# A fifth block of hidden gradients turned by a transposing load, and three PSUM copies moved from VectorE to ScalarE

## The chip, the cores and the metric

The kernel runs on one core of a Trainium2 chip. The metric is the device time of one execution in microseconds (us). The engines are named as in the profile: PE is TensorE's matmul stream and PEld its weight loads, DVE is VectorE, ACT is ScalarE, POOL is GpSimd, SP is SyncE, which here only issues DMAs; SPq is SP's queue, the instructions that SP works through in order. L1062 is line 1062 of the kernel file.

## The reference, cut to what matters

The function is the sum of its input, a gated convolution and a bilinear feed-forward block, and the kernel computes the output and all nine gradients.

```python
def _fwd_reference(A_q, A_k, A_v, A_shift_k, A_ssm_k, A_ssm_D, B_x, B_w_gate, B_w_up, B_w_down):
    # S = 2048 rows, D = 512 columns, F = 1376 hidden columns, bfloat16
    def _A_ref(q, k, v, shift_k, ssm_k, ssm_D):
        k_shift = sum(k_pad[:, t:t + S, :] * shift_k[:, 3 - t] for t in range(4))   # a 4-tap shift
        kv = k_shift * v
        y = irfft(rfft(kv) * rfft(ssm_k)) + kv * ssm_D                              # a long convolution
        return q * y
    def _B_ref(x, w_gate, w_up, w_down):
        return ((x @ w_gate) * (x @ w_up)) @ w_down
    xn = _layernorm(A_q)
    return A_q + _A_ref(xn, A_k, A_v, A_shift_k, A_ssm_k, A_ssm_D) + _B_ref(xn, B_w_gate, B_w_up, B_w_down)

out, vjp = jax.vjp(f, A_q, A_k, A_v, A_shift_k, A_ssm_k, A_ssm_D, B_w_gate, B_w_up, B_w_down)
return (out, *vjp(grad_out))
```

Of the outputs, these matter here: the weight gradients of the feed-forward block (out_7, out_8: D x F; out_9: F x D), the gradient of the four taps (out_4: 512 x 4), that of ssm_D (out_6: 512) and that of ssm_k (out_5).

## The kernel before, in words

The program has two halves. In the first (up to about 313 us of the profile) the feed-forward block is computed in eight chunks of 256 rows, and the convolution's spectra beside it. For each chunk the kernel keeps h (the product of gate and up) and the gradients dg and du, laid with the hidden columns on the partitions: three tiles of 128 hidden columns x 256 rows for each of the 11 blocks of hidden columns (ten of 128 and one of 96). Seven of the eight chunks go to the DRAM buffer HDD; the last stays on the chip in `hds[1]`.

The second half is the one that the change touches. Its backbone is `dw`, a loop over the 11 blocks `fb` (numbered from 0, so that `fb` 6 is the seventh and `fb` 8 the ninth). For each block `down_grad` multiplies h, turned so that rows lie on the partitions, with the output's gradient (`pd`, L1026, 16 matmuls; out_9), and then `pu` (L1062, 64 matmuls; out_7 and out_8) multiplies the normalized input with dg and du, turned as well. So each block needs 48 squares of 128 x 128 turned: h, dg and du, each with 16 groups of 128 rows. There are two ways to do it:

- `load_hb` loads a block as it lies into a buffer `hb`, and `hid_t(fb, t)` turns it on PE in three steps t = 0, 1, 2, each 16 transposes into a PSUM tile `pt` (L859) and one ACT copy into `nath` or `natd`. Steps 0 and 1 come ahead of the block's `pu`, right after the `down_grad` of the block before; step 2 sits in the middle of `down_grad` of the block itself.
- For the blocks in `TURNED`, before the change `fb` 7 to 10, `load_t` issues a transposing DMA from HDD into `natT` (L817). Only the last chunk is turned on PE, in `last_t`: 6 transposes (L829) and one ACT copy into a small tile `nat7`. `last_t(fb + 1)` comes in the middle of the `pu` of `fb`.

A block's load is issued two blocks ahead, from the middle of `down_grad(fb - 2)`. The buffers: `hb` has two, used in turn (and by `natT` of whole blocks); `natd` has two and `nath` one. The block `SPLIT` puts five chunks of its `natT` into a `natd` and two into the `nath`; the last block of 96 columns goes into a `natd`.

Beside the backbone run four side generators: after each `yield` of `dw` (six for a block, numbered n = 0, 1, 2, ...; block `fb` begins at n = 6 fb) a side whose turn has come does one step. `inv_y` (from n = 0, every third) brings the convolution's results back with `pq` and computes with DVE the products `dks` and `kb`; `dsk_gram` (from n = 27, every second) computes the taps' gradient; `inv_dk` (from n = 35, every third) writes out_5, and `put_dD` out_6; `ew` (from n = 10, every third) does the elementwise end on DVE, alternating `final(b)` and `bwd(b)` for eight row groups. `put_late` at the start of an `ew` step stores what the step before made (`o`, `e`, `dk`), and `final(b)` first loads `bb` of the next group. The tiles `o`, `e`, `dk` and `bb` have two buffers each.

`dsk_gram` makes, for each of four column groups c, a PSUM tile `pk` (L1085, 32 matmuls). DVE multiplies its two halves with an identity mask straight out of PSUM into `kd` (L1091), sums (L1093) and at the end turns the result on PE (`pts`, L1101) and copies it out into `dskt`; both `kd` and `dskt`, like `nat7`, live in the two buffers of the tag `dd`. PSUM has three large tiles (`P2`: `pt`, `pu`, `pk`, `po`, `pq` and others share them) and two small ones (`P1`: `pd`, `pts`, `ptd`). A tile is given to the next user when its copy-out is done.

The order within each engine's queue, SP's too, is planned when the program is built, by the program's order and by readiness in the planner's own model of time; the engines then work through their queues strictly in order. `tc.high_priority(offset=SOON)` lets an instruction go ahead of up to 300 others. `tc.issue_after(x)` puts an instruction behind x on x's queue: `behind(fb)` does so for some of the transposing loads.

Of the kernel before, what the change touches and what calls it, by code (L numbers as in the profile page):

```python
# [9 lines left out]
F32 = mybir.dt.float32  # L10
I32 = mybir.dt.int32
ALU = mybir.AluOpType
ACTF = mybir.ActivationFunctionType
AX = mybir.AxisListType
# [6 lines left out]
R = 16  # L21
P = 128
NC4 = 4
FBLK = [(i * 128, min(128, F - i * 128)) for i in range((F + 127) // 128)]
NFB = len(FBLK)
NCH = 8
SOON = 300
# [163 lines left out]
def kernel(  # L191
# [24 lines left out]
    nc = tc.nc  # L216
# [17 lines left out]
    def act(o, i):  # L234
        nc.scalar.copy(o, i)  # L235

    def dve(o, i):
        nc.vector.tensor_copy(o, i)  # L238
# [13 lines left out]
    def P2(name, shape, dt=F32):  # L252
        return ps2.tile(shape, dt, name=name, tag="p2")

    def P1(name, shape, dt=F32):
        return ps1.tile(shape, dt, name=name, tag="p1")

    ident = const.tile([P, P], BF, name="ident")
# [397 lines left out]
    first = ExitStack()  # L656
# [131 lines left out]
    LG = {}  # L788
# [6 lines left out]

    hbs = {}

    TURNED = range(NFB - 4, NFB)

    def behind(fb):  # L800
        first = {NFB - 2: lambda: LG["bb"], NFB - 1: lambda: LG["og"]}.get(fb)
        return tc.issue_after(first().ins) if first else ExitStack()

    def load_t(fb):

        f0, fw = FBLK[fb]
        if fb == SPLIT:
            parts = ((0, 5, "n", dict(tag="natd", bufs=2)), (5, NCH - 1, "n", dict(tag="nath")))
        elif fw < P:
            parts = ((0, NCH - 1, "n", dict(tag="natd", bufs=2)),)  # L810
        else:
            parts = ((0, NCH - 1, "b", dict(tag="hb")),)
        nats[fb, 0] = {}
        for a, e, pool, kw in parts:
            t = CP[pool].tile([P, e - a, 3, 2, fw], BF, name="natT", **kw)
            with behind(fb) as _, tc.high_priority(offset=SOON):
                nc.sync.dma_start_transpose(out=t[:].rearrange("s c t h f -> s (c t h) f"),  # L817
                                            in_=HDD[:fw, fb, a:e].rearrange("p c t s -> p (c t s)"))
            for c in range(a, e):
                nats[fb, 0][c] = t[:, c - a]  # L820

    SPLIT = NFB - 2

    def last_t(fb):
        f0, fw = FBLK[fb]
        pt = P2("pt7", [P, 3, 2, P], BF)
        for t in range(3):
            for h in range(2):
                nc.tensor.transpose(pt[:, t, h, :fw], hds[1][:fw, fb, t, h * 128:h * 128 + 128], ident[:fw, :fw])  # L829
        n7 = c2b.tile([P, 3, 2, P], BF, name="nat7", tag="dd")  # L830
        act(n7[:, :, :, :fw], pt[:, :, :, :fw])
        nats[fb, 1] = n7

    def nat_h(fb, r):
        f0, fw = FBLK[fb]
        if fb not in TURNED:
            return nats[fb, 0][:, r, :fw]
        return nats[fb, 0][r // 2][:, 0, r % 2, :] if r < R - 2 else nats[fb, 1][:, 0, r % 2, :fw]

    def nat_d(fb, r):  # L840
        f0, fw = FBLK[fb]
        if fb not in TURNED:
            return nats[fb, 1][:, :, r, :fw]
        return nats[fb, 0][r // 2][:, 1:3, r % 2, :] if r < R - 2 else nats[fb, 1][:, 1:3, r % 2, :fw]

    def hid_t(fb, t):
        if fb in TURNED:
            return
        f0, fw = FBLK[fb]
        hb = hbs.pop(fb) if t == 2 else hbs[fb]  # L850
        if t == 0:
            nats[fb, 0] = CP["n"].tile([P, R, P], BF, name="nath")
        elif t == 1:
            nats[fb, 1] = CP["n"].tile([P, 2, R, P], BF, name="natd", bufs=2)
        dst = nats[fb, 0] if t == 0 else nats[fb, 1][:, t - 1]
        pt = P2("pt", [P, R, P], BF)
        for r in range(R):
            hs = hb[:fw, r // 2, t] if r < R - 2 else hds[1][:fw, fb, t]
            nc.tensor.transpose(pt[:, r, :fw], hs[:, (r % 2) * 128:(r % 2) * 128 + 128], ident[:fw, :fw])  # L859
        act(dst[:, :, :fw], pt[:, :, :fw])  # L860
# [56 lines left out]
    c2b = ctx.enter_context(tc.tile_pool(name="c2b", bufs=2, side="right", reuse_waits="tile"))  # L917
# [8 lines left out]
    dsk = c2.tile([P, NC4, 4], F32, name="dsk")  # L926
# [15 lines left out]
    DKS = {}  # L942
# [46 lines left out]
    def inv_dk():  # L989
        o5t = c2.tile([P, NC4, P, R], BF, name="o5t", tag="o5k")  # L990
        o5 = out_5.rearrange("(c q) s -> c q s", q=P)
        for rq in range(4):
            gk = gks.pop(0)
            if rq == 0:
                gk_last = load_gk_last()
            for b in range(2):
                po = P2("po", [P, 2, 4, P])
                for h in range(2):
                    for i in range(4):
                        for c in range(2):  # L1000
                            nc.tensor.matmul(po[:, h, i, :], lhsT=(gk_last(c, i) if rq == 3 else gk[:, c, i])[:, cs(2 * b + h)], rhs=TB.IW[:, c, :],
                                             start=(c == 0), stop=(c == 1))
                act(o5t[:, 2 * b:2 * b + 2, :, 4 * rq:4 * rq + 4], po[:].rearrange("q h r s -> q h s r"))
                if b == 1 and rq < 2:
                    gks.append(load_gk(2) if rq == 0 else None)
                if rq == 3:
                    for c in (2 * b, 2 * b + 1):
                        nc.sync.dma_start(o5[c], o5t[:, c].rearrange("q s r -> q (s r)"))
                yield
            if rq == 0:  # L1010
                yield from put_dD(o5t)

    def put_dD(o5t):
        act(dDs[:], o5t[:, :, 0, 0])
        yield
        pt = P1("ptd", [P, P], BF)
        nc.tensor.transpose(pt[:NC4, :], dDs[:], ident[:])
        dDt = c2.tile([NC4, P], BF, name="dDt")
        dve(dDt[:], pt[:NC4, :])
        nc.sync.dma_start(out_6.rearrange("(c p) -> c p", p=128), dDt[:])  # L1020

    def down_grad(fb):
# [18 lines left out]
    def load_h(fb):  # L1041
        (load_t if fb in TURNED else load_hb)(fb)

    def dw():
        og = None
        load_hb(2)
        for fb, (f0, fw) in enumerate(FBLK):
# [12 lines left out]
            for c in range(NC4):  # L1060
# [3 lines left out]
                if c == 1:  # L1064
                    yield
                    if fb + 1 in TURNED:
                        last_t(fb + 1)
# [11 lines left out]
    def dsk_gram():  # L1079
        for c in range(NC4):  # L1080
            pk = P2("pk", [P, 2, D])
            for r in range(R):
                for h in range(2):
                    c0 = c * 128 + 64 * h
                    nc.tensor.matmul(pk[64 * h:64 * h + 64, h, 0:256], lhsT=dks[:, r, c0:c0 + 64],  # L1085
                                     rhs=KH[0][:, r:r + 4, c0:c0 + 64], start=(r == 0), stop=(r == R - 1))
            kd = c2b.tile([P, 4, 64], F32, name="kd", tag="dd")
            with tc.high_priority(offset=SOON):
                for h in range(2):
                    hs = slice(64 * h, 64 * h + 64)  # L1090
                    nc.vector.tensor_tensor(kd[hs], pk[hs, h, 0:256].rearrange("q (j c) -> q j c", j=4),  # L1091
                                            ident[hs, hs].unsqueeze(1).to_broadcast((64, 4, 64)), op=ALU.mult)
                nc.vector.tensor_reduce(dsk[:, c, :], kd[:], axis=AX.X, op=ALU.add)  # L1093
            yield
        dskb = c2.tile([P, 4, NC4], BF, name="dskb")
        nc.vector.tensor_copy(dskb[:], dsk[:].rearrange("q c i -> q i c"))
        for _ in range(2):
            yield
        pt = P1("pts", [P, 4, P], BF)
        for j in range(4):  # L1100
            nc.tensor.transpose(pt[:NC4, j, :], dskb[:, 3 - j, :], ident[:])  # L1101
        dskt = c2b.tile([NC4, P, 4], BF, name="dskt", tag="dd")
        dve(dskt[:], pt[:NC4].rearrange("c j q -> c q j"))
        nc.sync.dma_start(out_4.rearrange("(c p) j -> c p j", p=128), dskt[:])
        yield

# [88 lines left out]
    def load_dk():  # L1195
        gks.append(load_gk(0))
        gks.append(load_gk(1))
        yield

    sides = [every(seq(inv_y(), load_dk()), 0, 3), every(dsk_gram(), 27, 2), every(inv_dk(), 35, 3), every(ew(), 10, 3)]  # L1200
    for n, _ in enumerate(dw()):
        for sd in sides:
# [36 lines left out]
```

## Time and profile before

| What | Value |
|---|---|
| Median of three runs | 480.83 us (479.90 to 481.28) |
| The profiled execution's own time | 481.82 us |
| Its span, first to last instruction | 480.0 us |
| Granted PE clock | 0.999 |
| PE busy | 464.5 us, 97% |
| DVE, ACT busy | 340.5 us (71%), 305.6 us (64%) |
| Last PE matmul ends | about 475.9 us into the span |
| Last DVE work of the elementwise end ends | 471.8 us |

The profile is of one execution. Its parts: busy time by engine; the span in 40 slices; the DMA queues; the chain of work that ended last, followed back from the last instruction to what released each step; groups of like instructions; waits (who waited for whom, in us, how often, and the longest); and a timeline of each engine, with the idle time before an instruction in square brackets and what ended it. A DMA issue on SPq is shown with the time that SP was held by it; the time from issue to landing is shown apart.

### The profile page before, as it was taken

The page shows a single profiled execution, that of the slowest core. Times are in us where ns is not written, and L with a number is a line of the kernel's source. Part 1 is how long each engine was busy: PE and PEld are TensorE (multiplying, and loading weights), DVE is VectorE, ACT ScalarE, POOL GpSimd, SP SyncE. Part 2 cuts the span into 40 slices and gives each one's busy share as a digit, 9 for nine tenths or more (in the row PEclk, how much of TensorE's full clock was granted, in tenths as well). Part 3 has the DMA queues.
Part 4 walks back from the last instruction along what each step waited for, and adds up shares of the span by engine and source line. Part 5 has one row for each costly group of instructions (what it writes and reads, how often), then busy time and mean ns, then how long its engine had stood idle before and what let it go on. Part 6 is the DMA issues. An engine that isn't in the chain of part 4 may idle for free.

```text
span 480.0 us, 10366 instructions
## 1 busy us (share of the span) xinstructions
PE 464.5 (97%) x4252; PEld 311.6 (65%) x4293; DVE 340.5 (71%) x609; ACT 305.6 (64%) x349; POOL 14.0 (3%) x30
## 2 busy tenths in 40 slices
PE   7999999999999999999999999999999999999996
PEld 6867755547648447447447743576777687677885
DVE  7889989979366567686777877022257899599893
ACT  4957677659568678779779975375576535233141
POOL 8000000000000000000000000110000000000000
PEclk9999999999999999999999999999999999999999
DMA  8999999989998968968978379999899979999858
GB/s 268 374 381 366 310 296 320 315 300 328 318 288 270 277 202 255 285 200 245 298 235 259 118 272 331 388 329 313 312 361 364 371 260 320 318 267 239 252 155 294
DMA packets 111132, 139.85 MB, mean 291 GB/s; under 512 B 38859, under 2 KB 84336, under 8 KB 109550
## 3 DMA queue, kind: packets, MB, share of 16 engines
q1 hardware_dynamic: 109502, 137.85, 89.7%
q10 hardware_dynamic: 1584, 1.36, 1.0%
q8 instruction: 33, 0.54, 0.5%
q14 instruction: 13, 0.11, 0.1%
HBM read 67.08 MB, written 63.41 MB: 272 GB/s over the span
## 4 chain that ended last, share of the span: by engine, by line
PE 67%; DMA 15%; DVE 14%; issue 2%; SPq 2%; ACT 1%; DVEq 0%; ACTq 0%
PE px L555 15%; PE pgu L512 13%; PE pu L1062 8%; PE py L548 7%; PE pdh L518 6%; PE pd L1026 4%; PE ps L584 3%; DMA khC<-in_A_k_dram 3%; PE pg L613 3%; DMA ssk<-in_A_ssm_k_dram 2%; PE pf L370 2%; PE pt L859 2%; DMA vb<-in_A_v_dram 2%; DMA kb<-KS 2%; DMA x_b<-in_A_q_dram 2%
## 5 line engine op out<-in xcount | busy, mean ns | idle before, releaser
L555 PE MATMUL px<-WT,hd 128*128 128x512 bf16 (+1 forms) x340 | 78.6, 379 | 1.6 <-issue 1.4
L1062 PEld LDWEIGHTS <-xnC 128*128 128x128 bf16 x704 | 67.0, 98 | 8.4 <-issue 0.6
L555 PEld LDWEIGHTS <-hd 128*128 128x128 bf16 (+1 forms) x352 | 32.8, 98 | 44.4 <-issue 7.7
L235 ACT CAST gu<-pgu 128x1024 bf16<-128x1024 f32 (+1 forms) x48 | 45.4, 946 | 16.9 <-PE pgu L512 16.7
L235 ACT CAST GO<-pg 128x1024 bf16<-128x1024 f32 x48 | 46.2, 1015 | 13.8 <-issue 7.2
L235 ACT CAST SP<-ps 128x1024 bf16<-128x1024 f32 x47 | 45.5, 1025 | 13.7 <-PE ps L584 11.8
L512 PE MATMUL pgu<-xt,Wu 128*128 128x256 bf16 (+1 forms) x352 | 53.1, 273 | 1.1 <-DVE kn L238 0.6
L600 DVE TENSOR_TENSOR T<-SP 128x2048 bf16<-128x2048 bf16 x24 | 29.3, 1222 | 34.8 <-ACT SP L235 34.7
L512 PE MATMUL pgu<-xt,Wg 128*128 128x256 bf16 (+1 forms) x352 | 52.8, 273 | 0.0
L1062 PE MATMUL pu<-natd,xnC 128*128 128x256 bf16 x448 | 51.2, 273 | 0.0
L518 PE MATMUL pdh<-gt,WdT 128*128 128x256 bf16 (+1 forms) x352 | 46.9, 273 | 0.1
L235 ACT CAST fst<-pf 128x1024 bf16<-128x1024 f32 x44 | 42.7, 1031 | 5.5 <-issue 2.3
L512 PEld LDWEIGHTS <-Wu 128*128 128x128 bf16 (+1 forms) x352 | 33.0, 100 | 15.6 <-issue 10.7
L548 PE MATMUL py<-Wd,hd 128*128 128x512 bf16 (+1 forms) x167 | 40.2, 379 | 0.8 <-issue 0.5
L235 ACT CAST og<-pu 128x1024 bf16<-128x1024 f32 (+1 forms) x11 | 10.9, 993 | 43.7 <-PE pu L1062 28.3
L518 PEld LDWEIGHTS <-WdT 128*128 128x128 bf16 (+1 forms) x352 | 34.9, 100 | 4.8
L512 PEld LDWEIGHTS <-Wg 128*128 128x128 bf16 (+1 forms) x352 | 34.8, 100 | 3.7
L235 ACT COPY natd<-pt 128x2048 bf16<-128x2048 bf16 x14 | 26.2, 1875 | 12.0 <-PE pt L859 12.0
L533 DVE TENSOR_TENSOR hd<-gu,dh 128x1024 bf16<-128x1024 bf16 (+1 forms) x48 | 30.8, 641 | 0.8
L532 DVE TENSOR_TENSOR hd<-gu 128x512 bf16<-128x512 bf16 (+1 forms) x48 | 19.0, 397 | 16.7 <-ACT gu L235 16.7
L548 PEld LDWEIGHTS <-hd 128*128 128x128 bf16 (+1 forms) x176 | 16.5, 98 | 20.8 <-issue 3.1
L600 DVE TENSOR_TENSOR U<-SP 128x2048 bf16<-128x2048 bf16 x24 | 29.2, 1218 | 0.0
(177 smaller groups left out, 687.4 us busy)
## 6 DMA issues: line engine op xcount, KB each, us to landing
HDD<-hd SPq DMA_DIRECT2D x35, 384.0 KB, 4.5
FD<-fst SPq DMA_DIRECT2D x24, 512.0 KB, 4.9
X<-FD SPq DMA_DIRECT2D x24, 512.0 KB, 5.5
GD<-GO SPq DMA_DIRECT2D x24, 512.0 KB, 3.9
g<-GD SPq DMA_DIRECT2D x11, 1024.0 KB, 8.9
hb<-HDD SPq DMA_DIRECT2D x7, 1344.0 KB, 10.2
bb<-BX SPq DMA_DIRECT2D x8, 512.0 KB, 5.5
BX<-bx SPq DMA_DIRECT2D x7, 512.0 KB, 3.9
```

The source lines that it names most:

```text
L235: nc.scalar.copy(o, i)
L512: nc.tensor.matmul(pgu[:w, i, t, :], lhsT=W[:, c, f0:f0 + w], rhs=xt[:, :, c, :], start=(c == 0), stop=(c == NC4 - 1))
L518: nc.tensor.matmul(pdh[:w, i, :], lhsT=WdT[:, c, f0:f0 + w], rhs=gt[:, :, c, :], start=(c == 0), stop=(c == NC4 - 1))
L532: nc.vector.tensor_tensor(hd[:fw, fb0:fb0 + n, 0, :], gu[:fw, :n, 0, :], gu[:fw, :n, 1, :], op=ALU.mult)
L533: nc.vector.tensor_tensor(hd[:fw, fb0:fb0 + n, 1:3, :], gu[:fw, :n], dh[:fw, :n].unsqueeze(2).to_broadcast((fw, n, 2, 256)), op=ALU.mult)
L548: nc.tensor.matmul(py[:], lhsT=hd[:fw, fb, 0, ss], rhs=Wd[:fw, fb, :], start=(fb == 0), stop=(fb == NFB - 1))
L555: nc.tensor.matmul(px[:], lhsT=hd[:fw, fb, t, ss], rhs=W[:fw, fb, :], start=(t == 1 and fb == 0), stop=(t == 2 and fb == NFB - 1))
L584: nc.tensor.matmul(ps[32 * q:32 * q + 32, a, :], lhsT=TB.EF[64 * a:64 * a + 64, 4 * g + q, ri].rearrange("p k j -> p (k j)"), rhs=X[64 * a ...
L600: tt(W[:].rearrange("p c a d -> p c (a d)"), A[:, i:i + 1].rearrange("p c a d -> p c (a d)").to_broadcast((P, 2, 2 * D)), B[:].rearrange(" ...
L613: nc.tensor.matmul(pg[q // 2][64 * a:64 * a + 64, q % 2, :], lhsT=TB.EI[32 * q:32 * q + 32, 2 * g + a, yi].rearrange("p k c -> p (k c)"), ...
L1026: nc.tensor.matmul(pd[:fw, :], lhsT=nat_h(fb, r), rhs=goC[:, r, :], start=(r == 0), stop=(r == R - 1))
L1062: nc.tensor.matmul(pu[:, c, :, :fw], lhsT=xnC[:, r, cs(c)], rhs=nat_d(fb, r), start=(r == 0), stop=(r == R - 1))
```

## The change

The block `fb` 6 joins `TURNED`: its plain load and its three steps of `hid_t` go, and a transposing load, `last_t(6)` and one more `nat7` come. The split over `natd` and `nath` goes from `fb` 9 to `fb` 8, and `fb` 9 takes a whole `hb` buffer. `behind` gets two more entries: the load of `fb` 6 is placed behind the last load of `kb`, and that of `fb` 8 behind the last load of `load_gk_last`. In `dsk_gram` ACT now copies the two halves of `pk` out of PSUM into `kd` (one tile for two values of c), DVE multiplies in place from there, without the raised priority, and the turning of the result is two steps later (n = 43 rather than 39). The copies of `dskt` and `dDt` out of PSUM are done by ACT rather than DVE.

```diff
-    TURNED = range(NFB - 4, NFB)
+    TURNED = range(NFB - 5, NFB)
 
     def behind(fb):
-        first = {NFB - 2: lambda: LG["bb"], NFB - 1: lambda: LG["og"]}.get(fb)
+        first = {NFB - 5: lambda: DKS["kb", R - 2], NFB - 3: lambda: LG["gk"], NFB - 2: lambda: LG["bb"], NFB - 1: lambda: LG["og"]}.get(fb)
         return tc.issue_after(first().ins) if first else ExitStack()
...
-    SPLIT = NFB - 2
+    SPLIT = NFB - 3
...
         dDt = c2.tile([NC4, P], BF, name="dDt")
-        dve(dDt[:], pt[:NC4, :])
+        act(dDt[:], pt[:NC4, :])
...
-            kd = c2b.tile([P, 4, 64], F32, name="kd", tag="dd")
-            with tc.high_priority(offset=SOON):
-                for h in range(2):
-                    hs = slice(64 * h, 64 * h + 64)
-                    nc.vector.tensor_tensor(kd[hs], pk[hs, h, 0:256].rearrange("q (j c) -> q j c", j=4),
-                                            ident[hs, hs].unsqueeze(1).to_broadcast((64, 4, 64)), op=ALU.mult)
-                nc.vector.tensor_reduce(dsk[:, c, :], kd[:], axis=AX.X, op=ALU.add)
+            if c % 2 == 0:
+                kd = c2b.tile([P, 2, 4, 64], F32, name="kd", tag="dd")
+            for h in range(2):
+                hs = slice(64 * h, 64 * h + 64)
+                act(kd[hs, c % 2], pk[hs, h, 0:256].rearrange("q (j c) -> q j c", j=4))
+                nc.vector.tensor_tensor(kd[hs, c % 2], kd[hs, c % 2], ident[hs, hs].unsqueeze(1).to_broadcast((64, 4, 64)), op=ALU.mult)
+            nc.vector.tensor_reduce(dsk[:, c, :], kd[:, c % 2], axis=AX.X, op=ALU.add)
             yield
...
-        for _ in range(2):
+        for _ in range(4):
             yield
         pt = P1("pts", [P, 4, P], BF)
         for j in range(4):
             nc.tensor.transpose(pt[:NC4, j, :], dskb[:, 3 - j, :], ident[:])
         dskt = c2b.tile([NC4, P, 4], BF, name="dskt", tag="dd")
-        dve(dskt[:], pt[:NC4].rearrange("c j q -> c q j"))
+        act(dskt[:], pt[:NC4].rearrange("c j q -> c q j"))
```

## The prediction

> **What bounds the kernel now.** First the page's busy times: PE works 97% of the span, at a granted clock of 0.999, so the question is what PE still waits for and which of its work goes. The table of stretches then says where the idle is: between 410 and 420 us PE is busy 8.89 of 10 us, the only stretch after 314 us that loses over 0.3 us, before the work runs out.
>
> ```profile
> PE 464.5 (97%) x4252; PEld 311.6 (65%) x4293; DVE 340.5 (71%) x609; ACT 305.6 (64%) x349; POOL 14.0 (3%) x30
> ...
> 410.00:420.00 10.00, 8.89 (x86) 6.42 (x82) 5.22 (x14) 3.20 (x3) 0.00 (x0) 1.00 1.02 338
> ```
>
> Next PE's timeline. These are the three turning steps of `fb` 6 (the second and third wait for DVE, in brackets), and a `last_t` of a block that a transposing load turns:
>
> ```profile
> 400.69 0.94 PE L859 MATMUL pt<-ident,hb 128*128 128x128 bf16 x14
> 401.96 0.96 PE L859 MATMUL pt<-ident,hb 128*128 128x128 bf16 x14 [0.22 <-DVE kd L1091]
> 417.64 0.95 PE L859 MATMUL pt<-ident,hb 128*128 128x128 bf16 x14 [1.06 <-DVE kd L1091]
> 425.07 0.51 PE L829 MATMUL pt<-ident,hd 128*128 128x128 bf16 x6
> ```
>
> The chain of waits around that gap leads from PE through DVE's late `kd` to a late `bb` and to SP, which was held by a transposing load:
>
> ```profile
> 404.92 3.82 SPq L817
> ...
> 410.36 5.54 DMA bb<-BX
> ...
> 416.00 0.69 DVE o L1139
> ...
> 416.72 0.42 DVE kd L1091
> ```
>
> Last SP's queue, and what waited for stores in it. The plain load of `fb` 6 holds SP 0.64 us, the transposing one of `fb` 7 9.69:
>
> ```profile
> 391.28 0.64 SPq L793 DMA_DIRECT2D hb<-HDD  x1
> ...
> 399.05 9.69 SPq L817 DMA_TRANSPOSE natT<-HDD  x1
> ```
>
> ```profile
> 396.31 1.01 ACT L235 CAST og<-pu 128x1024 bf16<-128x1024 f32 x1 [7.90 <-DMA out_dram<-og]
> ```
>
> ```profile
> 413.62 0.69 DVE L1138 TENSOR_TENSOR o<-xnC,yC 128x1024 bf16<-128x1024 bf16 x1 [4.29 <-DMA out_dram<-o]
> ```
>
> So PE sets the end, but SP, held by transposing loads, is what makes DVE and ACT late, and these make PE wait. The change takes work from PE and puts a fifth such load on SP.
>
> **PE's work.** A group of 32 transposes takes 1.79 us in the chain, 0.056 us each. The 48 of `fb` 6 go: 2.69 us. `last_t(6)` adds 6: 0.33 us in the chain for another block. Net -2.35 us, all on PE, which has no cover; it counts in full.
>
> **The gram sums by ACT.** The two waits above (0.22 + 1.06 = 1.28 us) were for a PSUM tile that DVE had not yet read. Both waiting steps are gone, and the tile now comes free by ACT. A copy of 256 elements costs ACT 0.37 us (the half `od`, 96x256); bounds 0.37 and 0.59 (512 elements). I take 0.37, the same length: 8 x 0.37 = 3.0 us. Against that ACT loses three copies of 1.87 us and gains a `nat7` of 0.80, `dskt` (0.64 to 0.80 by the rows of 576 and 768 elements) and `dDt` (0.20, like `dDs`): about a microsecond less in all, on an engine at 20 to 50% there. DVE keeps eight multiplies, 0.42 us each from PSUM; from SBUF I leave them at that (0.3 to 0.45 by the sum's 0.41 over the same length), and loses `dskt` 0.68 and `dDt` 0.20. Cover for the loss of priority: `kd` of c = 1 must be summed before `nat7` of `fb` 6 may take its buffer, about 409 us; in program order it follows `final(3)`, which ended at 403.4, or 409 if DVE is 6 us late. PE needs that `nat7` only at row group 14 of `down_grad(6)`, near 416. Cost 0, a few us if that cover is gone. -1.28 us.
>
> [...]
>
> **The load of `fb` 6, on SP.** It goes behind the last `kb` load (issued 378.79) with raised priority, so I put it ahead of the stores `o`, `e` of group 1 (now 379.32 and 380.39) and of all up to `og`. It needs the buffer that `hid_t(4, 2)` leaves at 381.56. SP is then held 9.06 to 9.69 us (the two whole blocks of 128 in the trace): to 391.3. SP's cover is its own idle, about 7 us ahead of 387.96 and 4.6 ahead of 399.05. What is queued behind, with today's durations: `o`, `e`, `kb`, `dk`, `kb`, `bb` of group 3 by 393.9 (now 390.0), the two `og` stores by 395.0 (now 391.2), `od`, two loads `g` by 397.3 (now 394.4; first used at 413.8, landing in 8.9: covered). So SP is level again when the load of `fb` 7 can start, at 399.05, where its buffer comes free. Landing in about 11 us is far ahead of the use at 413.
>
> Who waits: ACT's `og` copy of `fb` 4 waits for those stores now (396.31); 3.8 us later it ends at 401.1. It holds a PSUM tile, and behind it stand two `kd` copies (0.74) and the `natd` copy of `hid_t(5, 2)` (1.76): done about 403.6. Without the two turning steps PE would begin `pu` of `fb` 5 at 402.6. Cost +1.0 us. The bounds: 0 if the `og` stores stay ahead; 4.3 if the load is put just ahead of `og` and behind `bb`, since then `og` lands near 404.5 and PE's `pk` at 400.7 has no tile. I take 1.0, for the priority.
>
> DVE: the store of `o` of group 1 lands at 391.4 + 4.5 = 395.9 (4.5 is the median of these stores), and DVE's L1138 of group 3 ran at 390.19: 5.7 us late. DVE then idles less at 409 to 416 (4.29 for `o` of group 2, 1.09 for `bb`), so most is made up: +0.3 us at 416.7, less the 0.88 of copies. DVE ends today at 471.8, 4.1 ahead of PE. Cost 0 as long as DVE ends within some 4 us of that.
>
> **The later loads.** `fb` 8 goes straight behind `load_gk_last` (418.2 to 419.2), about where it is (420.41); its two pieces hold SP as long as today's two of `fb` 9 (7.35 + 2.61). It now stands ahead of the store of `o` of group 4 (now 419.32), see the third rival. `fb` 9 as one piece starts after `bb` (433.3 today), lands by 446 and is used at 451; `fb` 10 is unmoved. 0 us each.
>
> **Two more steps of delay.** `pts` moves next to `ptd`, with nothing of PE's between but `po`. `ptd` then needs the small PSUM tile that `od` of `fb` 7 holds for 0.65 us after `down_grad(7)`; `pts` fills 0.33 of it. Today the gap at 432.5 is 0.1. Cost +0.2; bounds 0 and 0.6.
>
> **The sum.** -2.35 - 1.28 + 1.0 + 0.2 = -2.4 us. The profiled execution took 481.82 us (span 480.0); after it, 479.4. The median shown is 480.83, 1.0 below the profiled execution, so on the median: 478.4 us.
>
> [...]
>
> **The rivals.** 1: the stores stay ahead of the load, or its hold costs nobody (SP does idle 7 us there). -2.35 - 1.28 + 0.2 = -3.4: 477.4 us. Against it: the load of `fb` 7 did jump over `o`, `e`, `dk` and `bb` today.
>
> 2: the copies out of PSUM come no sooner, so the release by ACT does not do what it says: ACT stands behind `og` until 404.5. -2.4 + 3.3 = +0.9: 481.7 us, no measurable change (0.3%, 1.4 us, is about what can be told). For it: ACT already waited 7.90 us there.
>
> 3, slower: SP's holds make DVE end last. The price: 5.7 us at 390 by the load of `fb` 6, and 7.3 at 426.5, because `o` of group 4 is stored only when the load of `fb` 8 lets go (428.7) and lands at 433.8; 13.0 us. Off it: 0.9 of copies, 1.7 of today's wait at 447, and of the 5.4 idle at 409 to 416 half, since these stores slip too: 7.7 net, DVE ends at 479.5; its last `dk` needs 3.4 us to land, so the span is 482.9, +2.9: 483.7 us. It decides from DVE's end past 476.6 (480.0 - 3.4). For it: DVE has 99% of busy slices from 420 on. Against: the planner can put other work ahead of a waiting `o`. [...]
>
> **How the numbers follow.** The forecast 0.45, rival 1 0.15, rival 2 0.15, rival 3 0.25. Faster (below 479.4): the first two, 0.60; same: 0.15; slower (above 482.3): 0.25. The forecast's own range is 477.5 to 479.3; the whole one goes from 476.9 (rival 1 with the 0.2 and a little idle gone) to 482.7, which takes in rival 2 and the near edge of 3. No clock matters: it stays at 1.0.
>
> **What would show it.** L859 x16 fewer by three groups, L829 by one more; no PE wait for `kd`. The SP queue: six issues of L817, the first near 381.6, held 9 to 10 us. The ACT `og` copy of `fb` 4 near 400. DVE's L1138 of group 3 waiting for a store; its end between 471 and 474. Wrong it is if DVE ends after PE, if a `natT` lands late for its `pd`, or if `pts` waits for `dskb`.

## The result, and the profile after

The changed kernel takes 483.15 us (median of 12 runs, 480.63 to 486.29) where the kernel before takes 480.00 on the same chip (478.38 to 481.28): a ratio of 1.0063, 95% interval 1.0044 to 1.0081. It is slower, by some 3 us; 478.4 had been forecast, and the time lies above the range (476.9 to 482.7). The profiled execution took 484.33 us, with a span of 482.5 us.

The page's busy times, then the table of stretches (us; busy time of PE, PEld, DVE, ACT and POOL with their instructions; granted PE clock, as a share of full speed; DMA share; GB/s), both of the changed kernel:

```profile
PE 465.4 (96%) x4210; PEld 311.8 (65%) x4251; DVE 339.2 (70%) x607; ACT 304.2 (63%) x357; POOL 13.9 (3%) x30
```

```profile
410.00:420.00 10.00, 9.95 (x93) 7.63 (x92) 7.20 (x20) 4.41 (x6) 0.00 (x0) 1.00 0.99 331
...
440.00:450.00 10.00, 5.96 (x35) 3.77 (x34) 9.93 (x22) 4.13 (x5) 0.00 (x0) 0.71 1.11 268
```

The hole that the change was to close is closed: between 410 and 420 us PE is busy 9.95 us, not 8.89. PE has 42 matmuls fewer (4210 against 4252), which is 48 transposes out and 6 in. And yet PE's busy time has grown, from 464.5 to 465.4 us. The second row shows what is new: between 440 and 450 us PE stands idle for 4 us, and the granted clock is 0.71 on the mean of those 10 us; the matmuls behind the idle are busy for longer than the same ones in the kernel before (the 16 of `po` 1.71 us against 0.89). In the kernel before, this stretch was full:

```profile
440.00:450.00 10.00, 9.95 (x95) 7.63 (x95) 8.26 (x19) 3.53 (x4) 0.00 (x0) 1.00 1.14 259
```

The chain of waits leads through that hole (start, us, what; in order of time):

```profile
438.79 2.31 SPq L817
...
441.20 0.53 SPq L1034
...
441.82 3.07 DMA out_dram<-dskt
...
444.98 0.81 ACT nat L235
...
445.84 1.03 PE pd L1026 x2
446.87 1.71 PE po L1001 x16
448.58 4.73 PE pu L1062 x32
```

Read from the `pd` upwards: the last two matmuls of `down_grad(8)` (L1026) wait for the copy of `nat7` of `fb` 8 (L235); that copy waits for a store of `dskt`, 4 KB, to land; and that store waits in SP's queue behind `od` (L1034) and a transposing load (L817). Here are the two queues, SP's of the changed kernel and ACT's:

```profile
431.69 9.41 SPq L817 DMA_TRANSPOSE natT<-HDD  x1
441.20 0.53 SPq L1034 DMA_DIRECT2D out_dram<-od  x1
441.82 0.29 SPq L1104 DMA_DIRECT2D out_dram<-dskt  x1
```

```profile
429.51 0.57 ACT L235 COPY dskt<-pts 4x512 bf16<-4x512 bf16 x1
...
444.98 0.80 ACT L235 COPY nat<-pt 128x768 bf16<-128x768 bf16 x1 [13.37 <-DMA out_dram<-dskt]
```

`dskt` is copied at 429.51, and its store is issued only at 441.82, since the load of `fb` 9 stands ahead of it and holds SP for 9.41 us. `dskt` and `nat7` share the two buffers of the tag `dd`, so ACT sits idle for 13.37 us (the first 2.8 of them ahead of the end of `nat7`'s own transposes). In SP's queue of the kernel before, the store stood ahead of that load, and `nat7` waited only for its own transposes (SP, then ACT):

```profile
432.61 0.29 SPq L1104 DMA_DIRECT2D out_dram<-dskt  x1
...
433.80 10.00 SPq L817 DMA_TRANSPOSE natT<-HDD  x2
```

```profile
437.71 0.80 ACT L235 COPY nat<-pt 128x768 bf16<-128x768 bf16 x1 [2.81 <-PE pt L829]
```

The loss has two pieces. The first is PE's wait, 4.04 us, here in PE's timeline of the changed kernel and then the same two matmuls in the kernel before:

```profile
445.84 1.03 PE L1026 MATMUL pd<-goC,nat 128*128 128x512 bf16 x2 [4.04 <-ACT nat L235]
```

```profile
444.92 0.59 PE L1026 MATMUL pd<-goC,nat 128*128 128x512 bf16 x2
```

The second is the clock behind it. The stretches of a microsecond in the changed kernel:

```profile
444.00:445.00 1.00, 0.00 (x0) 0.00 (x0) 1.00 (x3) 0.02 (x1) 0.00 (x0) 0.58 1.07 402
...
447.00:448.00 1.00, 1.00 (x12) 1.00 (x11) 1.00 (x2) 1.00 (x2) 0.00 (x0) 0.50 0.92 300
...
450.00:451.00 1.00, 1.00 (x7) 0.69 (x6) 1.00 (x1) 0.00 (x0) 0.00 (x0) 0.51 1.26 166
451.00:452.00 1.00, 1.00 (x11) 0.90 (x10) 0.93 (x3) 0.00 (x0) 0.00 (x0) 1.00 1.94 125
```

From about 444.2 to 451.0 us the granted clock is 0.50, 6.8 us long. In the chain the two `pd` take 1.03 us, `po` 1.71 and `pu` 4.73, where the same groups take 0.59, 0.89 and 3.49 at full clock: 2.5 us more. Together 6.5 us. Up to the hole PE had gained: `down_grad(8)` begins at 438.83 us against 441.90 before, 3.1 us earlier (and about 3.6, since this execution entered the second half some 0.5 us later). 6.5 lost less 3.1 won is 3.4 us, and PE's last matmul ends at 479.24 us against 475.84: 3.4 us later.

These 6.5 us are those of an execution with a mean clock of 0.992. Of the twelve, five were at 0.992 (median 484.8 us), five at 0.996 (482.2) and two at 1.0 (480.63 and 482.2), so the part that the clock takes differs from one execution to the next.

### The profile page after: what moved, and what is told of

Its sections match the earlier page's. It is cut to its first block, busy times and chain, and to the rows that moved or that the text cites. A ratio compares the mean times of both kernels' runs of the same rounds, so it can differ in the third digit from the quotient of the medians.

```text
span 482.5 us, 10288 instructions
## 1 busy us (share of the span) xinstructions
PE 465.4 (96%) x4210; PEld 311.8 (65%) x4251; DVE 339.2 (70%) x607; ACT 304.2 (63%) x357; POOL 13.9 (3%) x30
## 4 chain that ended last, share of the span: by engine, by line
PE 69%; DMA 17%; DVE 8%; ACT 2%; issue 1%; SPq 1%; ACTq 0%; DVEq 0%
PE px L555 14%; PE pgu L512 12%; PE pu L1062 12%; PE py L548 7%; PE pdh L518 6%; PE pd L1026 4%; PE ps L584 3%; DMA khC<-in_A_k_dram 3%; PE pg L613 3%; DMA ssk<-in_A_ssm_k_dram 3%; PE pf L370 2%; DMA vb<-in_A_v_dram 2%; PE po L1001 2%; PE pt L859 2%; DMA kb<-KS 2%; DMA x_b<-in_A_q_dram 2%
## 5 line engine op out<-in xcount | busy, mean ns | idle before, releaser
L235 ACT CAST gu<-pgu 128x1024 bf16<-128x1024 f32 (+1 forms) x48 | 45.4, 946 | 17.0 <-PE pgu L512 16.6
L235 ACT CAST GO<-pg 128x1024 bf16<-128x1024 f32 x48 | 46.3, 1016 | 13.7 <-issue 7.2
L235 ACT CAST SP<-ps 128x1024 bf16<-128x1024 f32 x47 | 45.6, 1027 | 13.7 <-PE ps L584 11.8
L235 ACT CAST fst<-pf 128x1024 bf16<-128x1024 f32 x44 | 42.8, 1033 | 5.3 <-ACT fst L235 2.1
L1062 PE MATMUL pu<-natd,xnC 128*128 128x256 bf16 x384 | 43.9, 273 | 0.3 <-ACT natd L235 0.3
L1062 PE MATMUL pu<-natT,xnC 128*128 128x256 bf16 (+1 forms) x280 | 33.6, 274 | 0.0
L235 ACT CAST og<-pu 128x1024 bf16<-128x1024 f32 (+1 forms) x11 | 10.9, 993 | 27.7 <-PE pu L1062 24.6
```

The lines of the kernel that those rows point to most:

```text
L1062: nc.tensor.matmul(pu[:, c, :, :fw], lhsT=xnC[:, r, cs(c)], rhs=nat_d(fb, r), start=(r == 0), stop=(r == R - 1))
```

## The experiments

**Theory A** is the reading above: the store of `dskt`, moved behind the load of `fb` 9 in SP's queue, keeps the buffer that `nat7` of `fb` 8 needs. Its rivals are that the gain was never there (the copies by ACT, or the block turned by the load, cost what they save) and the others that stand with the runs. All ratios are against the kernel before on the same chip; each edit is against the changed kernel unless the text says otherwise.

### The buffer alone

`dskt` takes a buffer of another tag; the order of every queue stays as it is in the changed kernel.

```diff
-        dskt = c2b.tile([NC4, P, 4], BF, name="dskt", tag="dd")
+        dskt = c2b.tile([NC4, P, 4], BF, name="dskt", tag="od")
```

> The changed kernel with one edit: dskt takes the buffers of od instead of those of dd, so the small turned tile nat7 of fb 8 no longer shares a buffer with it. The planned order of every queue is the same as in the changed kernel. Theory A (the buffer): PE lost 4.0 us waiting for nat7 of fb 8, which waited for the store of dskt, which stood on SP behind the 9.4 us of the load of fb 9; and about 2.5 us more since PE ran at half clock for 6 us after that idle. Both go: ACT's nat7 of fb 8 follows its transposes at about 435, no PE wait over 0.5 us is left after 314 us, the clock stays at 1.0, the ratio to before is 0.990 to 0.994. Theory B (the queue): the fifth load's hold of SP makes DVE and ACT late and that is what costs; then nat7 is only the place where it shows, and the ratio stays above 1.000.

Measured: 477.48 us against 479.66, ratio 0.9948 (0.9925 to 0.9972), just above the range that A gave. SP's queue, then ACT's:

```profile
428.94 9.41 SPq L817 DMA_TRANSPOSE natT<-HDD  x1
...
439.07 0.29 SPq L1104 DMA_DIRECT2D out_dram<-dskt  x1
```

```profile
433.39 0.80 ACT L235 COPY nat<-pt 128x768 bf16<-128x768 bf16 x1 [2.82 <-PE pt L829]
```

The store is as late behind the load as it was (439.07, ten microseconds after the load's issue), but `nat7` no longer waits for it; PE's list of waits after 300 us is empty and the clock is 1.0. One word of the kernel is worth 1.1% (1.0063 to 0.9948), and what is left is a gain of 2.2 to 2.5 us (1.3 to 3.6 by the interval): the forecast's size.

### The turning of the sums two steps earlier

```diff
-        for _ in range(4):
+        for _ in range(2):
```

> The changed kernel with the turning of the taps' result two steps after the sums again, as in the kernel before, instead of four. The store of dskt then stands ahead of the load of fb 9 on SP. Theory A: no wait of nat7 of fb 8 for that store, no clock loss, and pts at about 421.7 does not wait, since dskb was ready at 416.3; ratio 0.990 to 0.995. Theory B: as the changed kernel, above 1.003.

Measured: 476.93 us against 479.66, ratio 0.9944 (0.9919 to 0.9970). `dskt` stays in `dd`. SP's queue:

```profile
427.62 0.46 SPq L1104 DMA_DIRECT2D out_dram<-dskt  x1
...
429.09 8.99 SPq L817 DMA_TRANSPOSE natT<-HDD  x1
```

With the two steps of delay taken back, the store stands ahead of the load again, and PE waits for nothing after 300 us. (`nat7` still waits 3.55 us for the store, ending at 434.4, which is ahead of PE's need.) So it is the delay in `dsk_gram` that moved the store, and not the changed places of the loads. This version and the one above are both faster than either kernel; they can't be told apart from one another.

### The store from ACT's own queue

```diff
-        nc.sync.dma_start(out_4.rearrange("(c p) j -> c p j", p=128), dskt[:])
+        nc.scalar.dma_start(out_4.rearrange("(c p) j -> c p j", p=128), dskt[:])
```

> The changed kernel with one edit: the store of dskt is issued by ACT, right behind its copy, rather than by SP; dskt keeps its buffer of the tag dd, which nat7 of fb 8 takes next. Theory A (it is SP's queue, held 9.4 us by the load of fb 9, that keeps the buffer): the store leaves at about 430 and lands by 433, nat7 of fb 8 follows its transposes without a wait for it, ratio 0.990 to 0.996, as with a buffer of its own. Rival C (sharing the buffer is enough, wherever the store is issued): a wait of nat7 stays, and the ratio is above 1.000.

Measured: 478.57 us against 480.13, ratio 0.9950 (0.9923 to 0.9976). ACT's queue:

```profile
432.88 0.68 ACTq L1104 DMA_DIRECT2D out_dram<-dskt  x1
433.60 1.01 ACT L235 CAST o5t<-po 128x1024 bf16<-128x1024 f32 x1 [1.33 <-DMA natT<-HDD]
436.94 0.80 ACT L235 COPY nat<-pt 128x768 bf16<-128x768 bf16 x1 [2.33 <-DMA out_dram<-dskt]
```

`dskt` and `nat7` share their buffers here, and the load of `fb` 9 stands where it stood. The store alone goes round it, and the gain is there. Theory A holds from three sides: the buffer, the order, the queue.

### `dskt` copied by DVE again

```diff
-        act(dskt[:], pt[:NC4].rearrange("c j q -> c q j"))
+        dve(dskt[:], pt[:NC4].rearrange("c j q -> c q j"))
```

> The changed kernel with one edit: dskt is copied out of PSUM by DVE again. The planned order of SP, ACT and PE is otherwise that of the changed kernel, the store of dskt behind the load of fb 9. Theory A: the copy's engine does not matter, the wait of nat7 of fb 8 for the store and the loss of clock stay: ratio 1.002 to 1.010. Rival D (the copy on ACT is what is late): the wait goes, ratio 0.990 to 0.996.

Measured: 483.08 us against 480.13, ratio 1.0067 (1.0047 to 1.0087): as slow as the changed kernel. PE's waits after 300 us:

```profile
PE pd L1026 <- ACT nat L235: 2.8, 1, 2.8
```

Which engine copies `dskt` doesn't matter; the store is late all the same (issued at 439.3 behind the load). In this profiled execution, the shortest of that kernel's five, the clock was 1.00 from 440 to 470 us although PE was idle there for 2.80 us; in the others the clock over the span was 0.992 or 0.996.

### A shorter load of `fb` 9

```diff
-            t = CP[pool].tile([P, e - a, 3, 2, fw], BF, name="natT", **kw)
+            e = 5 if fb == NFB - 2 else e; t = CP[pool].tile([P, e - a, 3, 2, fw], BF, name="natT", **kw)
...
-            for c in range(a, e):
-                nats[fb, 0][c] = t[:, c - a]
+            for c in range(a, NCH - 1 if fb == NFB - 2 else e):
+                nats[fb, 0][c] = t[:, (c - a) % (e - a)]
```

> The changed kernel with the load of fb 9 cut from seven chunks to five, 30 squares instead of 42: the rows of the last two chunks of that block are left out of its part of out_7, out_8 and out_9 (other chunks' rows stand in for them, with the same matmuls). Its hold of SP falls by 12 squares of 0.22 us, from 9.4 to about 6.7 us. Theory A: the store of dskt leaves 2.7 us sooner and PE's wait for nat7 of fb 8 falls from 4.0 to about 1.3 us. If the half clock is a fixed price of any idle, PE still runs slow for some 6 us after it and the ratio is 0.999 to 1.003; if it comes only after a long idle, the clock stays at 1.0 and the ratio is 0.993 to 0.998.

Measured: 479.05 us against 480.13, ratio 0.9970 (0.9933 to 1.0007). The kernel leaves the rows of two chunks of that block out of its three gradients; PE does the same number of matmuls. The ratio is lower than the changed kernel's, and its own spread is wide (476.53 to 482.56). It lies in the second of the two ranges expected, but the wait of about 1.3 us that the range rests on was not seen. The load held SP for 8.19 us in the profiled execution and not the 6.7 that 30 of 42 squares would give, so the hold did not shrink in proportion to the squares. That execution was the longest of ten, with a PE wait of 3.63 us and a stretch of 3.4 us at clock 0.50; eight of the ten had a clock of 0.998 or more. The direction is A's; the size is not settled by it.

### The gram part alone

The block's part is undone (`TURNED`, `behind` and `SPLIT` as before); the gram sums, `dskt` and `dDt` stay with ACT, and the delay stays.

```diff
-    TURNED = range(NFB - 5, NFB)
+    TURNED = range(NFB - 4, NFB)
...
-    SPLIT = NFB - 3
+    SPLIT = NFB - 2
```

> Only the part of the change in the gram sums: copies out of PSUM by ACT and the turning two steps later; the blocks 7 to 10 are turned by loads as before, fb 6 on PE. On SP the store of dskt stands behind both pieces of the load of fb 9 here too. Theory A: PE saves the 1.3 us of waits for kd, then waits for nat7 of fb 8 some 4 us (SP free at about 443.8, the store landing at 447, PE there at 443.6) and loses 2 to 3 us of clock: ratio 1.006 to 1.014. Theory B: without the fifth load nothing holds SP more than before: ratio 0.996 to 1.000.

Measured: 480.84 us against 479.66, ratio 1.0019 (0.9998 to 1.0040). The store stood behind the load of `fb` 9 here too, but in the profiled execution it came soon enough to cost PE only 0.6 us. SP's queue:

```profile
429.32 9.34 SPq L817 DMA_TRANSPOSE natT<-HDD  x2
...
439.85 0.29 SPq L1104 DMA_DIRECT2D out_dram<-dskt  x1
```

SP reached the load about 2.4 us earlier than in the changed kernel (429.32 against 431.69) and PE came to its need later, having 42 matmuls more. My sum for A had the store 4 us later than it was, so the expectation by A was too dark; and the gain of the other rival did not show either. Three of the twelve executions had a clock of 0.995 or 0.996, so PE may well have waited longer there; no profile shows it. The next run divides the two.

### The gram part alone, with the buffer freed

The kernel of the run above, with `dskt` in the tag `od` (the same line as in the first experiment).

> The gram part alone (block 6 still turned by the tensor engine, the ninth's load whole-but-split as before), with dskt in the buffers of od. Theory A (what took the gain of the gram part alone was again dskt's store behind the load of block 9, in the runs where it came later than in the profiled one): no run with a granted clock under 0.998, and the forecast's own term shows, -1.28 us: ratio 0.995 to 0.998. Rival E (the copies by ScalarE win nothing by themselves, dskt's buffer or not): ratio 1.000 to 1.003 as with the gram part alone.

Measured: 478.98 us against 480.50, ratio 0.9969 (0.9954 to 0.9984). No run's clock was under 0.999, and PE waits for nothing after 300 us. The gram part is worth 1.5 us (0.8 to 2.2 by the interval); the forecast's term for the copies by ACT was 1.28, and the run does not divide the copies from the rest of that part. `dskt`'s store took the gain away in the gram part alone as well.

### The turned block alone

The block's part stays; gram's sums, `dskt`, `dDt` and the delay are as before the change.

```diff
-            if c % 2 == 0:
-                kd = c2b.tile([P, 2, 4, 64], F32, name="kd", tag="dd")
...
-                act(kd[hs, c % 2], pk[hs, h, 0:256].rearrange("q (j c) -> q j c", j=4))
...
+            kd = c2b.tile([P, 4, 64], F32, name="kd", tag="dd")
+            with tc.high_priority(offset=SOON):
...
-        for _ in range(4):
+        for _ in range(2):
```

> Only the part of the change in the blocks: fb 6 turned by a load, the split at fb 8, the two new places in SP's queue; the gram sums, dskt and dDt as before. The store of dskt stands ahead of the load of fb 9. Theory A: PE saves 2.35 us of transposes and the two waits that stood before them, keeps 0.5 to 1.0 us of the wait for og and natd near 400, and may wait up to 1.3 us for kd at the tiles that come next; ratio 0.993 to 0.999. Theory B: the fifth load is the cost; ratio above 1.003.

Measured: 481.32 us against 479.66, ratio 1.0020 (0.9998 to 1.0043): no gain, though 42 matmuls are gone, and between the two expectations. The profiled execution (478.74 us, clock 1.0) shows PE waiting 1.84 us for `kd` at 413.6, in front of `po` (L1001). In 9 of the 12 runs the clock over the span was 0.996, and in one 0.993, which that profile doesn't explain. So the kernel was run once more for a profile of such a run.

> The kernel of turned_alone once more, for a profile of a run with a granted clock of 0.996, as most of its runs had. Theory A (the wait for kd, 1.84 us in the profile at clock 1.0, is longer in most runs and then costs clock): a PE wait for kd of 3 us or more near 412 to 418, and right behind it a stretch of about 3.3 us at a granted clock of 0.50. Rival F (the clock falls somewhere else, for another reason): the kd wait stays at 1 to 2.5 us and the stretch at 0.50 lies elsewhere.

Measured: 482.56 us, clock 0.996. The chain of waits of this execution, then its stretches of a microsecond:

```profile
409.39 0.12 SPq L817
...
409.56 4.73 DMA out_dram<-o
...
414.32 0.69 DVE o L1138
...
415.02 0.42 DVE kd L1091
...
416.03 1.05 PE po L1001 x16
417.08 5.14 PE pd L1026 x16
```

```profile
417.00:418.00 1.00, 1.00 (x6) 0.41 (x4) 1.00 (x3) 0.84 (x1) 0.00 (x0) 0.64 1.13 397
418.00:419.00 1.00, 1.00 (x4) 0.29 (x2) 1.00 (x5) 0.17 (x1) 0.00 (x0) 0.50 0.96 385
419.00:420.00 1.00, 1.00 (x4) 0.31 (x3) 1.00 (x3) 0.00 (x0) 0.00 (x0) 0.50 1.08 342
420.00:421.00 1.00, 1.00 (x5) 0.40 (x4) 1.00 (x6) 0.00 (x0) 0.00 (x0) 0.66 1.18 337
```

The old wait for `kd` has not gone with the transposes that used to wait there; it has moved to the next user of the PSUM tile, `po`, and PE, having less to do, comes to it sooner (at 413.3 us, against 416.6) and waits longer: 2.72 us here, against 1.06 in the kernel before. Behind it the clock is 0.50 for 3.4 us (the `pd` takes 5.14 us, and 3.45 in the profile of the run with the shorter load). The expected place of the loss of clock is right, the wait ahead of it is a little under the 3 us that I had named. So the block's part needs the gram part: alone it lengthens a wait that the gram part takes away. The gram part needs no partner, as the run before shows, but it brings the late store, and in the profiles PE waited longer for it where PE was earlier (4.04 us with the block's part, 0.6 without).

### The load of `fb` 6 further back

The changed kernel's PE loses 0.5 us near 400 behind the load of `fb` 6 (with the buffer freed, the profile shows no such wait). Is there anything to be had by another place for that load? It goes behind `og` of group 3.

```diff
-        first = {NFB - 5: lambda: DKS["kb", R - 2], NFB - 3: lambda: LG["gk"], NFB - 2: lambda: LG["bb"], NFB - 1: lambda: LG["og"]}.get(fb)
+        first = {NFB - 5: lambda: LG["og"], NFB - 3: lambda: LG["gk"], NFB - 2: lambda: LG["bb"], NFB - 1: lambda: LG["og"]}.get(fb)
...
-        dskt = c2b.tile([NC4, P, 4], BF, name="dskt", tag="dd")
+        dskt = c2b.tile([NC4, P, 4], BF, name="dskt", tag="od")
```

> The changed kernel with dskt in the buffers of od and the load of fb 6 placed behind the two og stores of fb 3 on SP instead of behind the last kb load, so that the stores of o and e, the load of bb and og go ahead of its 7 to 10 us. Theory A: the hold of SP by the load of fb 6 costs PE nothing once the buffer of nat7 is free: same time as with the buffer alone, ratio 0.992 to 0.998. Theory B (the hold costs): a further 0.5 to 1.0 us, ratio 0.001 to 0.002 lower, and ACT's og copy of fb 4 near 396.5 rather than 399.

Measured: 480.55 us against 480.13, ratio 1.0011 (0.9995 to 1.0028): the gain is gone, against both expectations, although PE waits for nothing after 300 us and its last matmul ends at 471.5, as with the buffer alone. SP's queue at the end, of this kernel and then of the one with the buffer alone:

```profile
390.16 7.14 SPq L817 DMA_TRANSPOSE natT<-HDD  x1
...
399.27 10.40 SPq L817 DMA_TRANSPOSE natT<-HDD  x1
...
470.72 1.18 SPq L1180 DMA_DIRECT2D out_dram<-dk  x1
472.00 2.29 SPq L1073 DMA_DIRECT2D out_dram<-og  x2
474.38 0.50 SPq L1039 DMA_DIRECT2D out_dram<-od  x1
```

```profile
467.38 0.71 SPq L1180 DMA_DIRECT2D out_dram<-dk  x1
468.98 1.66 SPq L1073 DMA_DIRECT2D out_dram<-og  x2
472.41 0.34 SPq L1039 DMA_DIRECT2D out_dram<-od  x1
```

Two loads now stand almost back to back (390.16 and 399.27), DVE's elementwise end comes at 469.5 instead of 465.7, and the last `dk` store pushes the two `og` stores and with them the last `od`, which is ready at 472.4, to 474.38. The span is 477.6 against 475.0 us. This is of the kind of the prediction's third rival (SP's holds make the last stores late), at the tail; the place of these 2.6 us is read from the two traces, and no run undid it by itself.

## Why the prediction was wrong

**The step that failed** is "Two more steps of delay". It priced one consequence, `ptd`'s wait for a small PSUM tile, at +0.2 us, and the measured cost of that was nothing: `po` fills the gap (chain of the changed kernel, no wait listed). The consequence that counted was not followed. Two steps of delay move every instruction of the side, its DMA too: the store of `dskt` was issued in the kernel before at 432.61 us, 1.2 us ahead of the load of `fb` 9 at 433.80, and any delay of more than that puts it behind a hold of 9 to 10 us. Nor did the prediction name who waits for the store: `nat7`, through the tag `dd`. It said in another place that `kd` and `nat7` share that buffer, and did not draw the line to `dskt`. In place of +0.2 us the runs show 6.5 us in the profiled execution, and 1.1% between the changed kernel and the one with the buffer freed.

**"No clock matters: it stays at 1.0"** failed with it. 2.5 of those 6.5 us are the clock after the wait.

**"The later loads … 0 us each"** was right on their own terms: `fb` 8's load was issued at 419.79 (forecast 418.2 to 419.2), `fb` 9's at 431.69 behind `bb`, and no `natT` landed late for its `pd`. As a hold on SP for what is queued behind, the load of `fb` 9 should have had the same account as that of `fb` 6: a list of the instructions behind it and of who waits for each.

**The rest of the sum fits.** With the buffer freed the change gives −2.5 us (0.9948 of 480; −1.3 to −3.6 by the interval) where −2.4 was forecast:

- The gram sums with the two steps of delay, −1.28 + 0.2 = −1.08: measured −1.5, −0.8 to −2.2 by the interval (gram part alone with the buffer freed). The ratio of 0.9969 speaks for the gram part with its copies here; the last tile is copied by ACT at 409.08 us in the changed kernel, and was read by DVE at 416.72 in the kernel before.
- PE's transposes with the load of `fb` 6, −2.35 + 1.0 = −1.35: the difference of the two kernels with the buffer freed is −1.0, give or take 1.3 us by their intervals, so the size fits and is not shown by itself. The order on SP was the one forecast. The queue of the changed kernel and ACT's `og` copy of `fb` 4:

```profile
378.69 0.43 SPq L939 DMA_DIRECT2D kb<-KS  x1
382.20 6.85 SPq L817 DMA_TRANSPOSE natT<-HDD  x1
389.16 0.51 SPq L1180 DMA_DIRECT2D out_dram<-o  x1
```

```profile
400.18 1.01 ACT L235 CAST og<-pu 128x1024 bf16<-128x1024 f32 x1 [3.15 <-DMA out_dram<-og]
```

  The hold was 6.85 us and not 9.06 to 9.69, the copy began at 400.18 as forecast, and PE lost 0.16 + 0.34 = 0.5 us by it in place of 1.0. Where the hold was 8.74 us, in the profile of the run with the store on ACT's queue, PE did lose 1.0 (0.7 + 0.3).
- DVE: its L1138 of group 3 was planned later and did not wait for the store; the elementwise end came at 467.7 us, ahead of the forecast 471 to 474. The third rival, which had the right sign and at 483.7 us nearly the measured 483.15, did not come about: its number would have been right by luck. (DVE's 99% from 420 us on, its support, leaves out 440 to 450, where DVE was busy 8.26 of 10 us in the kernel before.)

Of the other rivals, the first had the mechanism of the run with the buffer freed, whose profile shows nobody on PE waiting for the hold; its −3.4 us lies inside that run's interval, so the time does not part it from the forecast. The second fell, since the `kd` waits are gone from the changed kernel's list. None of the signs of being wrong that the prediction named came up; a late store was not among them.

## What to carry to other kernels

When a step is delayed, follow its DMA to the issuing queue and ask what it now stands behind, and then ask which later tile takes the buffer that the DMA reads; here a 4 KB store behind a transposing load cost 6.5 us in the profiled execution, more than the 48 transposes that the load saved (2.69 us at the 0.056 us each of the chain before). Holds of one queue want a list of everything behind them, for each load that moves and not for the new one alone. And removing work in front of a wait can make the wait longer (1.06 to 2.72 us here), so a cut on the bound engine may pay only together with what releases it (the turned block alone: ratio 1.0020).

## What the runs showed of the hardware

- After some idles of PE the granted clock was 0.50 for stretches of one length or twice that length. It was 3.4 us after waits of 2.72 us (the turned block, second profile) and 3.63 us (the shorter load), 6.8 us after 4.04 us (the changed kernel), and there was none after 1.84 us (the turned block, first profile: 1.00 from 410 to 430) and one wait of 2.80 us (`dskt` copied by DVE). Between 2.72 us with a loss and 2.80 without one the wait's length alone does not decide; what else does was not shown. The stretch did not begin with the end of the wait: in the changed kernel it began at about 444.2 us, before PE went on at 445.84, and in the second profile of the turned block at about 417.3, after PE had gone on at 416.03. The mean clocks of the changed kernel's executions, 0.992, 0.996 and 1.0, fit two, one and no such stretch; this is an estimate (3.4 us at 0.50 lose 1.7 us, 0.35% of 480). A mean clock alone did not say that PE's work was slowed: at 0.997 in the profile of the last run, the only stretch from 300 us on with less than 1.00 was the one from 470 us (0.74), in which PE's last matmul ended at 471.5.
- A transposing load of 42 squares of 128 x 128 held SP for 6.16 us in one profile (`fb` 6, the run with `dskt` copied by DVE) and for 10.76 us in another (`fb` 9, the run with the load further back), and one of 30 squares for 8.19. What sets the hold was not shown.
